# One PSUM tile per accumulator and per h, instead of tiles of two banks, in a fused attention and FFN kernel

## The chip, the cores and the metric

The kernel runs on one core of one Trainium2 chip. The metric is the time of one execution in device microseconds (us). The kernel before takes 1046.71 us in the median of three runs (1044.47 to 1053.35). Its engines are TensorE (PE, with the weight loads shown as PEld), VectorE (DVE), ScalarE (ACT), GpSimd (POOL) and SyncE (SP, which issues the transfers). Matrix products are written by PE into PSUM, eight banks of 512 fp32 per partition; DVE and ACT read them from there.

## The reference

Attention comes first: a pooled form over groups of four positions, repeated to full length, plus a local form with a band of three neighbours on each side. Its result is the input of a feed-forward network.

```python
def _attn_ref(q, k, v):                       # 8 batches x 8 heads x 576 x 64
    q_d, k_d, v_d = (t.reshape(B, H, Sd, 4, D).mean(axis=3) for t in (q, k, v))
    out_up = np.repeat(sm_attn(q_d, k_d, v_d), 4, axis=2)
    scores = np.where(np.abs(pos[:, None] - pos[None, :]) < 4, scale * q @ k.T, -1e9)
    return out_up + softmax(scores) @ v

def _moe_ref(x, w_in, w_out):                 # 4608 tokens, 512 -> 2048 -> 512
    h = x @ w_in
    g = np.where(h >= 1, h, np.where(h <= -1, 0.0, (h + 1) ** 2 / 4))
    return g @ w_out
```

All values are fp32. To keep their precision, each factor of the FFN's two products is held as a high and a low part, so that each product takes three matmuls (high by high, high by low, low by high).

## The kernel before, in words

**Tiling.** The 4608 tokens are cut into chunks: chunk 0 of 512 tokens, chunks 1 to 8 of 384, chunks 9 and 10 of 512. The 2048 inner columns are cut into 16 blocks f of 128. A *step* is one pair (chunk, f). In a step:

- the *first product* (`mm1`, matmuls at line 770) makes h of 128 x 384 or 128 x 512 in one PSUM bank, with 12 matmuls: four blocks of the inner dimension, three each;
- the *gate* (`gates`) makes g from h: ACT copies h from PSUM to m (line 789; in chunk 0 DVE reads h itself), DVE clamps (790), ACT squares (793), DVE combines (796), ACT writes the high part gh (803), POOL the low part gl (806);
- the *second product* (`mm2`, line 824) multiplies g by 128 rows of w_out and adds into the accumulators o0, o1, o2 (and o3 in chunks of 512), one bank each, with three matmuls for each. The accumulators stay in PSUM for the 16 steps of a chunk. After the last (f = 15) ACT copies each to osb (832), and SP sends it out.

**Stages.** Three stages follow one another.

- *First stage*: the attention of the first eight head pairs, the conversion of the weights and chunk 0, in an order written out by hand in the string `ORDER` under `manual_schedule`. A token such as `0.sl@hi1` names an operation and the PSUM tag of its tile; `f3.s2` is a quarter of a first product, `m1.0` the second product of f = 1 into o0.
- *Middle stage*: 128 first products, (1, 1) to (9, 0). The second product follows its first product by two steps: PE does `mm1(k)`, `mm2(k-2)`, `mm1(k+1)`, `mm2(k-1)`, and so on. At 25 places (`JOINS`) the attention of further head pairs is put in: in one step scores and weighted sums on PE (`join`, lines 560 to 615), softmax on DVE, POOL and ACT (631 to 682), and two steps later the transposes on PE (`turn_ps`, 702 and 704) with their copies on ACT (708, 712). These use a tile of four banks.
- *End stage*: the rest of chunks 9 and 10; the second product follows its first by one step. In chunks of 512 its order is o3, o0, o1, o2.

**PSUM before.** The pool `low` is open for the whole kernel, with two tags lo0 and lo1 of two banks each. In the first stage the pool `up` holds hi0 and hi1, in the middle stage `ps_g` takes those four banks, in the end stage `end` holds a new hi0. The function `bank` gives halves of them: h of even f is the first half of lo0, o0 the second half of lo0, o1 and o2 are the halves of lo1, o3 and the h of odd f are the halves of hi0. In the middle stage h is always the first half of lo0.

**Order and waits.** The program's framework tracks which instruction reads and writes which tile, and puts semaphore waits where another engine's earlier access has to be over. Each engine runs its instructions in order. In the middle and end stages the first matmul of each product is held in program order, so that PE's order is as the loops write it. The temporaries m, u, gh, gl and osb share ten buffers under one tag.

Of the kernel before, what the change touches and what calls it, by code (L numbers as in the profile page):

```python
# [9 lines left out]
F32 = mybir.dt.float32  # L10
# [7 lines left out]
P = 128  # L18
# [139 lines left out]
def attention_then_ffn(ctx: ExitStack, tc, qT, kT, vw, vp, vq, band, w_in, w_out, out):  # L158
# [25 lines left out]
    def load(n, name):  # L184

        if n == len(pairs):
            return
        b, p = pairs[n]
        if name in "qk" and n < NPAIR:
            t = wpool.tile([P, 1024], F32, name=f"first_{name}{n}", tag=f"w{'i' if name == 'q' else 'o'}{NFC - NPAIR + n}")  # L190
            nc.sync.dma_start(t[:, 0:S], (qT if name == "q" else kT)[b, p])
        elif name in "qk":
            t = apool.tile([P, S], F32, name=f"{name}_sb", tag=name, bufs=1)
            nc.sync.dma_start(t, (qT if name == "q" else kT)[b, p])
        elif name == "vp" and n < SECOND:
            t = scratch(n, "vp", [KB, 1024])
            nc.sync.dma_start(t, vp[b, p])
        elif name == "vp":
            t = apool.tile([P, FACTOR, P + D], F32, name="vq_sb", tag="vp", bufs=1)
            nc.sync.dma_start(t, vq[b - SECOND // NPAIR, p].rearrange("k (f c) -> k f c", f=FACTOR))  # L200
        else:
            t = scratch(n, "v", [P, NB * D]).rearrange("p (n d) -> p n d", n=NB)
            nc.sync.dma_start(t, vw[b, p].rearrange("k (n d) -> k n d", n=NB))
        loaded[name] = loaded[name, n] = t
# [329 lines left out]
    def pooled_sums(n):  # L534

        state["qd"], state["kd"] = first_qd, apool.tile([P, SD], F32, name="kd", tag="kd", bufs=1)
        for t, name in ((first_qd[:, 0:SD], "q"), (state["kd"], "k")):
            nc.vector.tensor_reduce(
                t, loaded[name].rearrange("p (s f) -> p s f", f=FACTOR), axis=AX.X, op=ALU.add
            )  # L540
# [180 lines left out]
    def load_weights(name, f):  # L721
        t = wpool.tile([P, 512, 2], I32, name=f"raw_{name}{f}", tag=f"w{name}{f}")
        nc.sync.dma_start(t, (w_in if name == "i" else w_out)[f].rearrange("p (n t) -> p n t", t=2))
        raw[name, f] = t
# [4 lines left out]
    def convert(name, f, piece):  # L729

        t = raw[name, f]
        if piece == 1:
            high = t.bitcast(F32)[:, :, 1]
            nc.scalar.activation(high, high, AF.Prelu, scale=2.0**-112, alpha=-(2.0**32))
        elif piece == 2:
            nc.scalar.activation(t[:, :, 0], t.bitcast(U32)[:, :, 0], AF.Copy, scale=2.0**-29)
        elif piece == 3:
            raw["m", name, f] = temp("m")
            mi = raw["m", name, f].bitcast(I32)
            nc.vector.tensor_scalar(mi, t[:, :, 1], 3, None, op0=ALU.logical_shift_left)  # L740
        elif piece == 4:
            mi = raw["m", name, f].bitcast(I32)
            nc.vector.tensor_tensor(mi, mi, t[:, :, 0], op=ALU.add)
        elif piece == 5:
            w = wpool.tile([P, 2, 512], F32R, name=f"w_{name}{f}", tag=f"w{name}{f}")
            nc.scalar.copy(w[:, 0], raw["m", name, f])
            weights[name, f] = w
        else:
            w = weights[name, f]
            nc.gpsimd.tensor_tensor(w[:, 1], raw["m", name, f], w[:, 0], op=ALU.subtract)  # L750

    places = {}
# [28 lines left out]
    def gate(c, f, piece):  # L781

        size = CHUNKS[c][1]
        h = htiles[c, f]
        if piece == "u1":
            utiles[c, f] = temp("u")[:, :size]
            if c > 0:
                m = utiles["m"] = temp("m")[:, :size]
                nc.scalar.copy(m, h)  # L789
            nc.vector.tensor_scalar(utiles[c, f], m if c > 0 else h, -1.0, 1.0, op0=ALU.max, op1=ALU.add)  # L790
        elif piece == "sq":
            u = utiles[c, f]
            nc.scalar.activation(u, u, AF.Square, scale=0.5)  # L793
        elif piece == "u2":
            u = utiles[c, f]
            nc.vector.scalar_tensor_tensor(  # L796
                u, utiles["m"] if c > 0 else h, 1.0, u, op0=ALU.max, op1=ALU.min
            )
        elif piece == "gh":
            gh = mpool.tile([P, 512], F32R, name="gh", tag="t512", bufs=10)[:, :size]  # L800
            gl = mpool.tile([P, 512], F32R, name="gl", tag="t512", bufs=10)[:, :size]
            gtiles[c, f] = gh, gl
            nc.scalar.copy(gh, utiles[c, f])  # L803
        else:
            gh, gl = gtiles[c, f]
            nc.gpsimd.tensor_tensor(gl, utiles.pop((c, f)), gh, op=ALU.subtract)  # L806

    def gates(c, f):
        with tc.high_priority(offset=100):
            for piece in ("u1", "sq", "u2", "gh", "gl"):  # L810
                gate(c, f, piece)
# [25 lines left out]
        for t in (3, 0, 1, 2) if CHUNKS[c][1] == 512 else (0, 1, 2):  # L837
            second_product(c, f, t)

    low = ctx.enter_context(tc.tile_pool(name="low", bufs=1, space=bass.MemoryType.PSUM))  # L840
    banks = {}

    def bank(pool, tag, i):
        if tag not in banks:
            banks[tag] = pool.tile([P, 2, 512], F32, name=f"ffn_{tag}", tag=tag)
        return banks[tag][:, i]

    with tc.tile_pool(name="up", bufs=1, space=bass.MemoryType.PSUM) as up, tc.manual_schedule():
        ops = [first_pairs(n) for n in range(SECOND)]
        ops.append({f"l{x}": lambda x=x: load(SECOND, {"p": "vp"}.get(x, x)) for x in "qkpv"})  # L850
        warm = up.tile([P, 2, 512], F32, name="warm", tag="hi1")
        for _ in range(WARM):
            nc.tensor.matmul(warm[:, 0, 0:P], ident, ident, start=True, stop=True)
        places["h"] = lambda f: bank(up, "hi0", 1) if f % 2 else bank(low, "lo0", 0)
        places["o"] = lambda t: (
            bank(low, "lo0", 1), bank(low, "lo1", 0), bank(low, "lo1", 1), bank(up, "hi0", 0)
        )[t]
        for token in ORDER:
            token, _, tag = token.partition("@")
            whose, what = token.split(".")  # L860
            kind, f = whose[0], whose[1:]
            if kind in "io":
                if what == "ld":
                    load_weights(kind, int(f))
                else:
                    convert(kind, int(f), int(what[1]))
            elif kind == "f":
                c, f = divmod(int(f), NFC)
                if what[1:].isdigit() and what[0] == "s":
                    product(c, f, int(what[1]))  # L870
                else:
                    gate(c, f, what)
            elif kind == "m":
                second_product(0, int(f), int(what))
            elif tag:
                ops[int(whose)][what](low if tag[0] == "l" else up, tag)
            else:
                ops[int(whose)][what]()
    steps = [(c, f) for c in range(1, len(CHUNKS)) for f in range(NFC)]
    first, second = iter(steps[1:]), iter(steps)  # L880
    gates(*steps[0])
    with tc.tile_pool(name="ps_g", bufs=1, space=bass.MemoryType.PSUM) as ps_g:
        places["h"] = lambda f: bank(low, "lo0", 0)
        pooled_sums(SECOND)
        joined = None
        for n in range(NFC + 1, (NMID + 1) * NFC + 1):
            mm1(*next(first))
            if n in JOINS:
                joined = join(SECOND + JOINS.index(n), ps_g)
                next(joined)  # L890
                next(joined, None)
            elif n - 1 in JOINS:
                next(joined, None)
            if n > NFC + 1:
                mm2(*next(second))
            if n - 2 in JOINS:
                next(joined, None)
        mm2(*next(second))
    with tc.tile_pool(name="end", bufs=1, space=bass.MemoryType.PSUM) as end:
        del banks["hi0"]  # L900
        places["h"] = lambda f: bank(end, "hi0", 1) if f % 2 else bank(low, "lo0", 0)
        places["o"] = lambda t: (
            bank(low, "lo0", 1), bank(low, "lo1", 0), bank(low, "lo1", 1), bank(end, "hi0", 0)
        )[t]
        for c, f in first:
            mm1(c, f)
            mm2(*next(second))
        for c, f in second:
            mm2(c, f)
# [65 lines left out]
```

## Time and profile before

| | |
|---|---|
| median of three runs | 1046.71 us (1044.47 to 1053.35) |
| profiled execution | 1048.52 us, span of its trace 1046.7 us |
| PE busy / weight loads | 930.7 us (89%) / 791.4 us (76%) |
| DVE / ACT / POOL busy | 476.1 / 466.6 / 379.0 us |
| mean granted clock of PE | 0.991 |
| first products, 128x384 and 128x512 into lo0, high parts | 310.9 us, 1216 matmuls |
| second products, high parts, into lo0 and lo1 | 332.1 us, 1056 matmuls |

A row of the timeline has start and duration in us, engine, line, operation, the tile written and what it reads, the shape, the number of merged instructions, and in brackets how long the engine sat idle before it and what ended that. A row of the waits has who waited for whom, the sum in us, how often and the longest. A row of the chain has start, duration and what the chain was in. Matmuls are pipelined: each lasts longer than the distance to the next one's start, so rates are read from starts.

### The profile page before, as it was taken

How to read it: one execution, taken by the hardware profiler on the slowest of the kernel's cores; microseconds unless marked ns; L12 is line 12 of the kernel's file. 1: busy time of each engine (PE TensorE's matmuls, PEld its weight loads, DVE VectorE, ACT ScalarE, POOL GpSimd, SP SyncE). 2: the span in 40 equal slices, each digit the busy share in tenths (PEclk: the TensorE clock that was granted, in tenths of full speed). 3: DMA queues.
4: the chain of work that ended last, by engine and by line, in shares of the span. 5: the costliest groups of instructions: out<-in, count | busy, mean ns of one | idle time of the engine just before them, and what ended most of it. 6: DMA issues, size and time to landing. Idle time of an engine off the chain costs nothing.

```text
span 1046.7 us, 18187 instructions
## 1 busy us (share of the span) xinstructions
PE 930.7 (89%) x7444; PEld 791.4 (76%) x7444; DVE 476.1 (45%) x866; ACT 466.6 (45%) x987; POOL 379.0 (36%) x356
## 2 busy tenths in 40 slices
PE   8689999998998999899898899799989989998997
PEld 6577777787877877777787778688877877776775
DVE  5877945654533454354354255545555421211121
ACT  5889844444434434444443344444444432323233
POOL 5566654433422443233233233333333322121211
PEclk9899999999999999999999999999999999999999
DMA  9883103212111111211111011121121000001001
GB/s 286 291 296 134 52 17 110 67 56 77 51 38 43 52 51 51 68 51 51 46 51 52 31 51 51 51 82 51 51 81 52 14 31 1 1 0 41 1 1 40
DMA packets 27970, 68.56 MB, mean 66 GB/s; under 512 B 3248, under 2 KB 3248, under 8 KB 27888
## 3 DMA queue, kind: packets, MB, share of 16 engines
q1 hardware_dynamic: 27888, 67.42, 19.4%
q8 instruction: 58, 0.95, 0.4%
q14 instruction: 24, 0.20, 0.1%
HBM read 57.97 MB, written 9.44 MB: 64 GB/s over the span
## 4 chain that ended last, share of the span: by engine, by line
PE 61%; ACT 13%; issue 10%; DVE 10%; POOL 5%; DMA 0%; POOLq 0%; ACTq 0%; SPq 0%; DVEq 0%
PE ffn_lo L824 26%; PE ffn_lo L770 20%; ACT m L789 6%; PE ffn_hi L770 5%; DVE u L796 4%; POOL sl L638 3%; ACT sp L666 2%; PE ffn_hi L824 2%; POOL gl L806 2%; PE turn_ps L702 1%; ACT sl L664 1%; ACT osb L832 1%; PE turn_ps L704 1%; DVE sl L682 1%; ACT gh L803 1%
## 5 line engine op out<-in xcount | busy, mean ns | idle before, releaser
L824 PE MATMUL ffn_lo<-w_o,gh 128*128 128x512 f32 x1056 | 332.1, 396 | 80.3 <-ACT m L789 59.4
L806 POOL TENSOR_TENSOR gl<-u,gh 128x384 fp32r<-128x384 f32 (+1 forms) x176 | 194.1, 1103 | 569.5 <-ACT gh L803 398.9
L770 PE MATMUL ffn_lo<-xh,w_i 128*128 128x384 f32 (+1 forms) x1216 | 310.9, 338 | 0.8 <-ACT m L789 0.6
L824 PEld LDWEIGHTS ffn_lo<-w_o,gh 128*128 128x128 f32 x1056 | 187.3, 189 | 146.4 <-ACT m L789 97.1
L790 DVE TENSOR_SCALAR u<-m 128x384 f32<-128x384 f32 (+1 forms) x160 | 60.4, 378 | 419.3 <-ACT m L789 419.2
L770 PEld LDWEIGHTS ffn_lo<-xh,w_i 128*128 128x128 f32 x1216 | 217.8, 190 | 12.7 <-ACT m L789 0.9
L770 PE MATMUL ffn_lo<-xl,w_i 128*128 128x384 f32 (+1 forms) x608 | 203.7, 335 | 0.0
L824 PE MATMUL ffn_lo<-w_o,gl 128*128 128x512 f32 x528 | 200.8, 380 | 0.0
L803 ACT CAST gh<-u 128x384 fp32r<-128x384 f32 (+1 forms) x176 | 95.1, 541 | 135.2 <-DVE u L796 133.4
L796 DVE SCALAR_TENSOR_TENSOR u<-m,u 128x384 f32<-128x384 f32 (+1 forms) x160 | 116.0, 725 | 83.8 <-ACT u L793 83.8
L789 ACT COPY m<-ffn_lo 128x384 f32<-128x384 f32 (+1 forms) x144 | 70.4, 489 | 179.9 <-PE ffn_lo L770 179.9
L793 ACT ACTIVATE u<-u 128x384 f32<-128x384 f32 (+1 forms) x176 | 97.5, 554 | 99.7 <-DVE u L790 99.6
L770 PEld LDWEIGHTS ffn_lo<-xl,w_i 128*128 128x128 f32 x608 | 115.2, 190 | 2.5
L824 PEld LDWEIGHTS ffn_lo<-w_o,gl 128*128 128x128 f32 x528 | 100.3, 190 | 14.2
L770 PE MATMUL ffn_hi<-xh,w_i 128*128 128x512 f32 x192 | 59.1, 391 | 0.6 <-DVE u L796 0.6
L529 POOL TENSOR_TENSOR xl<-x,xh 128x576 fp32r<-128x576 f32 (+4 forms) x32 | 44.1, 1386 | 36.2 <-ACT xh L528 36.1
L664 ACT ACTIVATE sl<-sl 128x640 f32<-128x640 f32 x24 | 17.7, 737 | 63.0 <-POOL sl L638 63.0
L770 PEld LDWEIGHTS ffn_hi<-xh,w_i 128*128 128x128 f32 x192 | 37.1, 195 | 6.8 <-DVE u L796 1.4
L824 PE MATMUL ffn_hi<-w_o,gh 128*128 128x512 f32 x96 | 30.3, 397 | 11.6 <-ACT m L789 11.6
L770 PE MATMUL ffn_hi<-xl,w_i 128*128 128x512 f32 x96 | 37.2, 387 | 0.0
L638 POOL TENSOR_TENSOR sl<-sl,mxl 128x640 f32<-128x640 f32 x24 | 30.3, 1261 | 6.0 <-DVE mxl L637 6.0
L824 PEld LDWEIGHTS ffn_hi<-w_o,gh 128*128 128x128 f32 x96 | 16.7, 189 | 19.7 <-ACT m L789 18.0
(146 smaller groups left out, 1014.5 us busy)
## 6 DMA issues: line engine op xcount, KB each, us to landing
v<-vw SPq DMA_DIRECT2D x29, 320.0 KB, 3.0
vq_sb<-vq SPq DMA_DIRECT2D x24, 384.0 KB, 3.1
out<-osb SPq DMA_DIRECT2D x36, 256.0 KB, 2.4
raw_i<-w_in SPq DMA_DIRECT2D x16, 512.0 KB, 8.6
raw_o<-w_out SPq DMA_DIRECT2D x16, 512.0 KB, 9.4
q_sb<-qT SPq DMA_DIRECT2D x28, 288.0 KB, 4.3
k_sb<-kT SPq DMA_DIRECT2D x28, 288.0 KB, 4.9
vp<-vp SPq DMA_DIRECT2D x5, 288.0 KB
```

What stands on the lines that cost most here:

```text
L529: nc.gpsimd.tensor_tensor(xl[:, p, dst], x[:, part], xh[:, p, dst], op=ALU.subtract)
L638: shifted = nc.gpsimd.tensor_tensor(slf, slf, ml.unsqueeze(2).broadcast_to([P, NB, WIN]), op=ALU.subtract)
L664: nc.scalar.activation(slf, slf, AF.Exp, scale=0.125)
L666: nc.scalar.activation(sp[:, i], sp_v[i], AF.Exp, bias=mx[:, j : j + 1], scale=scale, accum_out=sums[:, NB + i : NB + i + 1],)
L770: ins = nc.tensor.matmul(htiles[c, f], wi[:, wt, cc * P : (cc + 1) * P], turns(xt[:, cc, ts]), start=(cc == 0 and xt is xh and wt == 0), s ...
L789: nc.scalar.copy(m, h)
L790: nc.vector.tensor_scalar(utiles[c, f], m if c > 0 else h, -1.0, 1.0, op0=ALU.max, op1=ALU.add)
L793: nc.scalar.activation(u, u, AF.Square, scale=0.5)
L796: nc.vector.scalar_tensor_tensor(u, utiles["m"] if c > 0 else h, 1.0, u, op0=ALU.max, op1=ALU.min)
L803: nc.scalar.copy(gh, utiles[c, f])
L806: nc.gpsimd.tensor_tensor(gl, utiles.pop((c, f)), gh, op=ALU.subtract)
L824: ins = nc.tensor.matmul(o, gt[:, ts], turns(weights["o", f][:, wt, :]), start=f == 0 and n == 0, stop=f == NFC - 1 and n == 2,)
```

## The change

Each accumulator and each h gets a PSUM tile of its own of one bank, made by the new function `single`; the tiles of two banks remain for the attention of the first stage. The pool `low`, open throughout, goes. In the first stage a pool `three` holds the tags lo0, lo1 and hi0 for the attention, and is closed at the first token of the FFN; a pool `six` with h0, h1, o0 to o3 is opened in the place of its banks. The middle stage opens `ps_g` (four banks) and `ffn` (h0, o0, o1, o2), the end stage `end` with six tiles. The gate of step (1, 0) is issued inside the first stage's block. The string `ORDER`, the loops, the operations and their shapes are the same.

```diff
-    low = ctx.enter_context(tc.tile_pool(name="low", bufs=1, space=bass.MemoryType.PSUM))
     banks = {}
 
-    def bank(pool, tag, i):
-        if tag not in banks:
-            banks[tag] = pool.tile([P, 2, 512], F32, name=f"ffn_{tag}", tag=tag)
-        return banks[tag][:, i]
-
-    with tc.tile_pool(name="up", bufs=1, space=bass.MemoryType.PSUM) as up, tc.manual_schedule():
+    def single(pool, *tags):
+        for tag in tags:
+            banks[tag] = pool.tile([P, 512], F32, name=f"ffn_{tag}", tag=tag)
+        places["h"] = lambda f: banks["h1" if f % 2 and "h1" in banks else "h0"]
+        places["o"] = lambda t: banks[f"o{t}"]
+
+    def psum(name):
+        return tc.tile_pool(name=name, bufs=1, space=bass.MemoryType.PSUM)
+
+    with psum("pair") as two, tc.manual_schedule(), ExitStack() as six:
...
-        places["h"] = lambda f: bank(up, "hi0", 1) if f % 2 else bank(low, "lo0", 0)
-        places["o"] = lambda t: (
-            bank(low, "lo0", 1), bank(low, "lo1", 0), bank(low, "lo1", 1), bank(up, "hi0", 0)
-        )[t]
+        three = six.enter_context(psum("three"))
         for token in ORDER:
...
             elif kind == "f":
                 c, f = divmod(int(f), NFC)
+                if not banks:
+                    six.close()
+                    single(six.enter_context(psum("six")), "h0", "h1", "o0", "o1", "o2", "o3")
...
             elif tag:
-                ops[int(whose)][what](low if tag[0] == "l" else up, tag)
+                ops[int(whose)][what](two if tag == "hi1" else three, tag)
...
+        gates(1, 0)
...
-    gates(*steps[0])
-    with tc.tile_pool(name="ps_g", bufs=1, space=bass.MemoryType.PSUM) as ps_g:
-        places["h"] = lambda f: bank(low, "lo0", 0)
+    banks.clear()
+    with psum("ps_g") as ps_g, psum("ffn") as four:
+        single(four, "h0", "o0", "o1", "o2")
...
-    with tc.tile_pool(name="end", bufs=1, space=bass.MemoryType.PSUM) as end:
-        del banks["hi0"]
-        places["h"] = lambda f: bank(end, "hi0", 1) if f % 2 else bank(low, "lo0", 0)
...
+    with psum("end") as end:
+        single(end, "h0", "h1", "o0", "o1", "o2", "o3")
```

On every engine the instructions stand in the same order as before, but for one place on DVE, where two neighbours at the head of the middle stage change places. What differs is the semaphore waits. Two places on PE show how; PE's rows read line, operation, tile written, what it reads (first and second product by the weights w_i and w_o), shape, count, and the engines waited for.

The first place is the last step of a chunk in the middle stage: the end of a first product, the second product with f = 15 into o0, o1, o2, and the start of the next first product. Before (ffn_lo_605 is lo0 with h and o0, ffn_lo_731 is lo1 with o1 and o2):

```order
L770 MATMUL ffn_lo_605<-xl,w_i_601 128x384
L824 MATMUL ffn_lo_605<-w_o_1608,gh 128x512 [waits Activation_49]
L824 MATMUL ffn_lo_605<-w_o_1608,gh 128x512
L824 MATMUL ffn_lo_605<-w_o_1608,gl 128x512 [waits Pool_49]
L824 MATMUL ffn_lo_731<-w_o_1608,gh 128x512 x2
L824 MATMUL ffn_lo_731<-w_o_1608,gl 128x512
L824 MATMUL ffn_lo_731<-w_o_1608,gh 128x512 [waits Activation_49]
L824 MATMUL ffn_lo_731<-w_o_1608,gh 128x512
L824 MATMUL ffn_lo_731<-w_o_1608,gl 128x512
L770 MATMUL ffn_lo_605<-xh,w_i_824 128x384 x2
```

The same place now (ffn_h_1871 is h0; ffn_o_1872, 1873 and 1874 are o0, o1 and o2):

```order
L770 MATMUL ffn_h_1871<-xl,w_i_601 128x384
L824 MATMUL ffn_o_1872<-w_o_1615,gh 128x512 x2
L824 MATMUL ffn_o_1872<-w_o_1615,gl 128x512 [waits Pool_49]
L824 MATMUL ffn_o_1873<-w_o_1615,gh 128x512 x2
L824 MATMUL ffn_o_1873<-w_o_1615,gl 128x512
L824 MATMUL ffn_o_1874<-w_o_1615,gh 128x512 x2
L824 MATMUL ffn_o_1874<-w_o_1615,gl 128x512
L770 MATMUL ffn_h_1871<-xh,w_i_831 128x384 [waits Activation_49]
```

Two waits for ACT are gone: the one at the head of the second product (for the copy of h to m) and the one ahead of o2 (for the copy of o1 to osb). A wait for ACT stands now at the head of the next first product (for the copy of h to m). In steps with other f only the first of the two was there, and has moved in the same way.

The second place is a step of the end stage with even f: before (ffn_hi_8529 is hi0 with o3 and the h of odd f):

```order
L770 MATMUL ffn_lo_605<-xl,w_i_1597 128x512
L824 MATMUL ffn_hi_8529<-w_o_1614,gh 128x512 [waits Activation_49]
L824 MATMUL ffn_hi_8529<-w_o_1614,gh 128x512
L824 MATMUL ffn_hi_8529<-w_o_1614,gl 128x512 [waits Pool_49]
L824 MATMUL ffn_lo_605<-w_o_1614,gh 128x512 [waits Activation_49]
L824 MATMUL ffn_lo_605<-w_o_1614,gh 128x512
L824 MATMUL ffn_lo_605<-w_o_1614,gl 128x512
```

And now (ffn_o_8550 is o3, ffn_o_8547 is o0):

```order
L770 MATMUL ffn_h_8545<-xl,w_i_1604 128x512
L824 MATMUL ffn_o_8550<-w_o_1621,gh 128x512 [waits Activation_49]
L824 MATMUL ffn_o_8550<-w_o_1621,gh 128x512
L824 MATMUL ffn_o_8550<-w_o_1621,gl 128x512 [waits Pool_49]
L824 MATMUL ffn_o_8547<-w_o_1621,gh 128x512 x2
L824 MATMUL ffn_o_8547<-w_o_1621,gl 128x512
```

The waits ahead of o3 for gh and gl remain. The wait ahead of o0, for the copy of this step's h to m, is gone. In steps with odd f it stood ahead of o3 instead (there h lay in hi0), and is gone too.

More of the change, by code (lines that the diff above doesn't have):

```diff
@@ L838, in mm2 @@
             second_product(c, f, t)
-    low = ctx.enter_context(tc.tile_pool(name="low", bufs=1, space=bass.MemoryType.PSUM))
     banks = {}
-    def bank(pool, tag, i):
-        if tag not in banks:
-            banks[tag] = pool.tile([P, 2, 512], F32, name=f"ffn_{tag}", tag=tag)
-        return banks[tag][:, i]
-    with tc.tile_pool(name="up", bufs=1, space=bass.MemoryType.PSUM) as up, tc.manual_schedule():
+    def single(pool, *tags):
[6 more added lines that the diff above has]
+    with psum("pair") as two, tc.manual_schedule(), ExitStack() as six:
         ops = [first_pairs(n) for n in range(SECOND)]
         ops.append({f"l{x}": lambda x=x: load(SECOND, {"p": "vp"}.get(x, x)) for x in "qkpv"})
-        warm = up.tile([P, 2, 512], F32, name="warm", tag="hi1")
+        warm = two.tile([P, 2, 512], F32, name="warm", tag="hi1")
         for _ in range(WARM):
             nc.tensor.matmul(warm[:, 0, 0:P], ident, ident, start=True, stop=True)
-        places["h"] = lambda f: bank(up, "hi0", 1) if f % 2 else bank(low, "lo0", 0)
-        places["o"] = lambda t: (
-            bank(low, "lo0", 1), bank(low, "lo1", 0), bank(low, "lo1", 1), bank(up, "hi0", 0)
-        )[t]
+        three = six.enter_context(psum("three"))
         for token in ORDER:
@@ L898, in attention_then_ffn @@
         mm2(*next(second))
-    with tc.tile_pool(name="end", bufs=1, space=bass.MemoryType.PSUM) as end:
-        del banks["hi0"]
-        places["h"] = lambda f: bank(end, "hi0", 1) if f % 2 else bank(low, "lo0", 0)
-        places["o"] = lambda t: (
-            bank(low, "lo0", 1), bank(low, "lo1", 0), bank(low, "lo1", 1), bank(end, "hi0", 0)
-        )[t]
+    with psum("end") as end:
+        single(end, "h0", "h1", "o0", "o1", "o2", "o3")
         for c, f in first:
```

## The prediction

> **What bounds the kernel now.** I read the page first, for the busiest engine, then the waits of PE over the run, then the chain and the timeline of single steps.
>
> ```profile
> PE 930.7 (89%) x7444; PEld 791.4 (76%) x7444; DVE 476.1 (45%) x866; ACT 466.6 (45%) x987; POOL 379.0 (36%) x356
> ```
>
> PE is busy for 89% of the span and no engine beside it for half of it (PEld is its own weight loads), so the question is what keeps PE idle. The waits of its second products, and one row of its weight loads:
>
> ```profile
> PE ffn_lo L824 <- ACT m L789: 59.4, 103, 0.7
> PE ffn_lo L824 <- ACT osb L832: 17.5, 11, 3.2
> PE ffn_hi L824 <- ACT m L789: 11.6, 16, 0.7
> PEld ffn_lo L824 <- ACT m L789: 97.1, 118, 1.1
> ```
>
> 103 times a second product waits for the copy of h out of the other half of lo0: in the middle stage, in all steps but those where the attention's matmuls stand between. None of these waits is for data: the copy to m belongs to the step whose first product has just ended, and the second product behind it works on g of two steps ago. The chain of waits over one such step, in order of time:
>
> ```profile
> 623.86 2.21 PE ffn_lo L824 x9
> 626.07 1.96 PE ffn_lo L770 x12
> 628.04 0.02 issue
> 628.06 0.49 ACT m L789
> ...
> 628.59 2.21 PE ffn_lo L824 x9
> ```
>
> A step takes 628.59 - 623.86 = 4.73 us, and for half a microsecond of it PE stands still for ACT. How fast PE goes without a wait is read from starts in the timeline, from a second product into a first one:
>
> ```profile
> 604.50 0.59 PE L824 MATMUL ffn_lo<-w_o,gh 128*128 128x512 f32 x2
> 605.15 0.60 PE L824 MATMUL ffn_lo<-w_o,gh 128*128 128x512 f32 x2
> 605.79 0.49 PE L770 MATMUL ffn_lo<-xh,w_i 128*128 128x384 f32 x2
> 606.28 0.49 PE L770 MATMUL ffn_lo<-xh,w_i 128*128 128x384 f32 x2
> ```
>
> Three matmuls of 512 columns take 0.65 us, three of 384 take 0.49 us, and the passage from one product to the other costs nothing extra.
>
> **The change part by part.** The instructions keep their order, so only waits are counted.
>
> *Copy of h, middle stage.* Without the wait a step is 4 x 0.49 + 3 x 0.65 = 3.91 us, 0.82 us less than 4.73. The idle time is 59.4 / 103 = 0.58 us of that; the other 0.25 us is what a restart costs (the last matmul's own length, and the first weight load). 103 x 0.82 = **84.5 us**.
>
> What is late next? The wait that is new stands at the head of the next first product, for the same copy. PE gets there a whole second product (1.95 us) later, and the copy is over 0.55 us after its product. Behind it on PE stands everything, but it has 1.4 us of room. Then gh and gl: a second product needs those of two steps ago, two steps being 7.8 us. Steps with the softmax are the tight ones. Of one, whose first product ends at 601.6, the timeline and the chain show:
>
> ```profile
> 604.38 1.00 POOL L806 TENSOR_TENSOR gl<-u,gh 128x384 fp32r<-128x384 f32 x1 [3.83 <-issue]
> 607.96 0.47 ACT L789 COPY m<-ffn_lo 128x384 f32<-128x384 f32 x1
> 608.48 0.70 PE L824 MATMUL ffn_lo<-w_o,gh 128*128 128x512 f32 x2 [0.57 <-ACT m L789]
> 612.30 0.55 DVE L241 TENSOR_TENSOR sp<-sp,sums 128x384 f32<-128x384 f32 x1
> 612.67 0.48 ACT L789 COPY m<-ffn_lo 128x384 f32<-128x384 f32 x1
> 612.83 1.00 POOL L806 TENSOR_TENSOR gl<-u,gh 128x384 fp32r<-128x384 f32 x1 [1.04 <-ACT gh L803]
> 615.41 0.66 PE turn_ps L702 x6
> ```
>
> gl is ready at 605.38, 3.8 us after its product, and in the next step, with DVE and ACT in the softmax, at 613.83, 5.9 us after the product that the copy at 607.96 follows; both inside 7.8. Two waits go ahead of the transposes (those behind the copies at 607.96 and 612.67), so the transposes would start 1.64 us earlier, at about 613.7. They need sp, last written at 612.85: 0.8 us of room. The first product behind them needs the copy that ends at 613.15, and would start near 614.9: 1.7 us of room. In the sum new stalls count 0; up to 0.3 us for each of 24 attention blocks (7 us) goes into the range.
>
> *Copy of an accumulator.* At the end of a chunk o2 waits until o1 is copied, behind gh on ACT. The real need comes a first product later (1.96 us), when the next chunk writes o0, whose copy ends earlier still. Of 17.5 us in 11 waits the last, of 0.68, is in the tail below: 16.8 + 10 restarts x 0.25 = **19.3 us**.
>
> *Copy of h, end stage.* With even f the accumulator o3 goes first and hides most of the copy; with odd f nothing does:
>
> ```profile
> 872.66 0.38 PE L824 MATMUL ffn_hi<-w_o,gl 128*128 128x512 f32 x1
> 873.12 0.70 PE L824 MATMUL ffn_lo<-w_o,gh 128*128 128x512 f32 x2
> 877.54 0.38 PE L770 MATMUL ffn_hi<-xl,w_i 128*128 128x512 f32 x1
> 878.65 0.70 PE L824 MATMUL ffn_hi<-w_o,gh 128*128 128x512 f32 x2 [0.73 <-ACT m L789]
> ```
>
> From start to start stand 0.46 and 1.11 us where 0.215 would; with 0.11 us for the first pair (0.70 against 0.59) the loss is 0.35 and 1.00. Odd: 16 waits, the last not counted (tail): **15.0 us**. Even: the weight loads wait 118 times, 103 of them above, so 15 x 0.35 = **5.3 us**.
>
> *The tail*, the last second product (o3, o0, o1, wait, o2) and its copies:
>
> ```profile
> 1034.61 0.58 ACT L789 COPY m<-ffn_hi 128x512 f32<-128x512 f32 x1 [2.37 <-PE ffn_hi L770]
> 1039.21 0.48 PE L824 MATMUL ffn_hi<-w_o,gl 128*128 128x512 f32 x1 [0.68 <-POOL gl L806]
> 1040.44 1.18 ACT L832 COPY osb<-ffn_lo 128x512 f32<-128x512 f32 x2
> 1041.67 0.70 PE L824 MATMUL ffn_lo<-w_o,gh 128*128 128x512 f32 x2 [0.68 <-ACT osb L832]
> 1042.68 0.58 ACT L832 COPY osb<-ffn_lo 128x512 f32<-128x512 f32 x1 [1.06 <-PE ffn_lo L824]
> ```
>
> The last gl follows its product by about 4.6 us, whatever PE does between: so the last odd wait brings nothing. (In the steps before, PE needs gl 5.17 + 0.43 = 5.6 us after the product: 1 us of room.) Without the wait for osb the last copy starts at 1041.62, behind the other two: **1.1 us**.
>
> *The clock.* After two long waits PE ran slowly for a while. One, in the chain and in stretches of 5 us (the numbers at the end: granted clock, transfers' share, GB/s):
>
> ```profile
> 947.39 0.70 PE L824 MATMUL ffn_lo<-w_o,gh 128*128 128x512 f32 x2 [2.47 <-ACT osb L832]
> 948.31 4.29 PE ffn_hi L770 x12
> 961.69 2.60 PE ffn_hi L770 x12
> 425.00:430.00 5.00, 4.38 (x22) 3.90 (x21) 0.92 (x2) 2.33 (x5) 0.00 (x0) 0.87 0.11 41
> 950.00:955.00 5.00, 4.27 (x16) 3.29 (x15) 0.94 (x2) 1.21 (x2) 0.00 (x0) 0.81 0.16 57
> ```
>
> 4.29 - 2.60 = 1.7 us, and the same for the stretch at 425: **3.4 us**, if it is the wait that slows PE. [...]
>
> *First stage.* One wait is longer, one goes:
>
> ```profile
> 36.83 0.70 PE L770 MATMUL ffn_lo<-xh,w_i 128*128 128x512 f32 x2
> 37.05 0.74 DVE L490 TENSOR_TENSOR own<-pl_ps,own 128x576 f32<-128x576 f32 x1
> 68.24 0.70 PE L824 MATMUL ffn_lo<-w_o,gh 128*128 128x512 f32 x2 [2.24 <-DVE u L796]
> ```
>
> h0 lies where hi0 was, whose last reader is the DVE row, so PE's first FFN matmul starts at 37.8: 1 us lost. At 68.24 two accumulations (1.3 us) now go ahead of the wait, and the next product into h0 waits. Net 0, between -2 and +2.
>
> Sum: 84.5 + 19.3 + 15.0 + 5.3 + 1.1 + 3.4 + 0 = 128.6 us. The profiled execution took 1048.5 us (span 1046.7), so it becomes 919.9; the median of the runs lies 1.8 us lower: **918 us**.
>
> **The rivals.**
>
> *Softmax sets the pace of the attention blocks.* If sp comes over 0.8 us later than traced (the copies on ACT and the matmuls now collide with it), the excess is lost at each of 24 blocks, up to both waits gained there, 24 x 1.64 = 39 us: 957 us; with half of it, 938. For it: the chain at these places runs through DVE, ACT and POOL already. Against: that chain hangs on the block's own matmuls, which start it no sooner relative to it, and the row at 601 to 613 has its room. 0.08 for about half, 0.05 for all.
>
> *Slower: the clock.* PE would run 747 us (918 less the first 160 and 11 of the tail) with almost no pause. If the granted clock there fell below 747 / (747 + 128.6) = 0.853, the kernel would be slower than before; at the 0.81 of the row above it would take 918 + 747 x 0.23 = 1090 us. Against it: within a step PE runs 4 us without a pause already, and the clock over the 100 us from 600 is full:
>
> ```profile
> 600.00:700.00 100.00, 88.75 (x821) 77.24 (x820) 49.88 (x94) 41.35 (x97) 37.03 (x37) 1.00 0.20 62
> ```
>
> 0.03. [...]
>
> *The waits are not what PE stands on.* If PE, let through, waited at the same places for gh or gl, nothing would change: 1047. The two steps of distance speak against it. 0.02.
>
> **How the numbers follow.** Forecast 0.82 with 918. Its own bounds: new stalls +7, the clock +3.4, the first stage +-2, a step read 0.02 us too short or long (103 times, +-2): 912 to 931. The half case at 938 belongs to the range of 8 in 10: **912 to 938**; outside are the full softmax case, the clock and no change. A run of this kernel tells 1% from no change; faster by more: 0.82 + 0.08 + 0.05 = 0.95; same 0.02; slower 0.03.
>
> **What would show it.** Right: no row of PE's second products waiting for m or osb but for a few; a middle step of 3.9 us in the chain; PE busy near 97% of a shorter span; the end stage's pair of steps 10.3 us instead of 11.7; no drop of the clock after 60 us. Wrong: transposes (702) waiting for DVE's sp, first products (770) waiting for m, join matmuls waiting for the copies at 708 and 712, a granted clock under 0.95, or a step of 3.9 us with matmuls spaced wider than 0.163 and 0.215 us.

## The result and the profile after

The kernel after takes 925.97 us in the median of four runs (922.49 to 927.31), against 1046.43 us before (the three runs above and one more); the ratio is 0.8833, with a 95% interval of 0.8785 to 0.8882. The forecast was 918 us, in a range of 912 to 938. The profiled execution took 924.72 us with a span of 922.9, 123.8 us less than the span before, where the sum of the prediction had 128.6.

The page, and the rows in which PE waits after the change (engine, line and tile, who was waited for, the sum in us, how often, the longest):

```profile
PE 891.7 (97%) x7444; PEld 792.2 (86%) x7444; DVE 477.3 (52%) x866; ACT 460.9 (50%) x987; POOL 380.5 (41%) x356
...
PE tp_ps L438 <- DVE sl L395: 8.4, 2, 6.6
...
PE turn_ps L702 <- DVE sp L241: 1.2, 1, 1.2
PE ffn_h L770 <- ACT m L789: 1.2, 3, 0.6
PE join_ps L560 <- POOL gl L806: 1.1, 2, 0.5
...
PE ffn_h L770 <- ACT osb L832: 0.7, 1, 0.7
...
PE ffn_o L824 <- ACT osb L832: 0.3, 1, 0.3
```

The same instructions, 7444 matmuls, fill 97% of a shorter span. Of the second products' waits for m, 71 us in 119 places before, none is left; for the copies to osb 0.3 us is left of 17.5; the wait for m that is new at the head of the next first product shows three times. A wait of the first product for osb is new as well (0.7 us, at the head of the end stage). The largest row that remains (8.4 us) lies in the first stage and was there before, with 8.1. The chain, first over two steps of the middle stage, then over an even and an odd step of the end stage:

```profile
555.74 1.94 PE ffn_o L824 x9
557.68 1.95 PE ffn_h L770 x12
559.63 1.94 PE ffn_o L824 x9
561.57 1.95 PE ffn_h L770 x12
```

```profile
771.77 2.59 PE ffn_o L824 x12
774.36 2.59 PE ffn_h L770 x12
776.95 2.59 PE ffn_o L824 x12
779.54 2.59 PE ffn_h L770 x12
```

Neither ACT nor "issue" stands between the products any more. A step takes 3.89 us in place of 4.73, a pair of steps at the end 10.36 in place of 11.71. The stretches in which the two places fall now where the clock had dropped, and the whole middle stage (PE busy, PEld, DVE, ACT, POOL, granted clock, transfers' share, GB/s):

```profile
150.00:750.00 600.00, 595.00 (x5383) 543.23 (x5382) 326.20 (x616) 283.93 (x661) 243.71 (x233) 1.00 0.19 63
385.00:390.00 5.00, 5.00 (x33) 4.62 (x32) 2.02 (x4) 3.04 (x7) 1.86 (x2) 1.00 0.04 12
836.00:841.00 5.00, 5.00 (x25) 4.38 (x24) 0.96 (x2) 3.78 (x7) 1.28 (x1) 1.00 0.28 103
```

PE pauses for 5 us of 600, and the clock is full.

Since PE runs the same instructions in the same order in both kernels, the two traces can be laid side by side product by product. The difference by stage, in us (the end stage begins with the first product of step (9, 1), the tail with the last wait of the last second product for gl):

| stage | terms of the prediction | predicted | measured |
|---|---|---|---|
| first stage (to 155.9 us before) | | 0 | -0.3 |
| middle stage | copy of h 84.5, osb 16.6, clock 1.7 | -102.8 | -98.1 |
| end stage | odd 15.0, even 5.3, osb 2.7, clock 1.7 | -24.7 | -24.5 |
| tail | | -1.1 | -0.9 |
| sum | | -128.6 | -123.8 |

### The profile page after: what moved, and what is told of

Same layout as the page of the kernel before. It is cut to its first block, busy times and chain, and to the rows that moved or that the text cites. A ratio compares the mean times of both kernels' runs of the same rounds, so it can differ in the third digit from the quotient of the medians.

```text
span 922.9 us, 18189 instructions
## 1 busy us (share of the span) xinstructions
PE 891.7 (97%) x7444; PEld 792.2 (86%) x7444; DVE 477.3 (52%) x866; ACT 460.9 (50%) x987; POOL 380.5 (41%) x356
## 4 chain that ended last, share of the span: by engine, by line
PE 83%; DVE 6%; ACT 5%; issue 3%; POOL 2%; DMA 1%; POOLq 0%; ACTq 0%; DVEq 0%
PE ffn_h L770 36%; PE ffn_o L824 35%; PE join_ps L572 2%; PE join_ps L587 1%; PE turn_ps L702 1%; PE join_ps L598 1%; PE turn_ps L704 1%; PE join_ps L560 1%; POOL sl L638 1%; DVE u L796 1%; ACT sp L666 1%; PE tp_ps L438 1%; POOL xl L529 1%; ACT osb L832 1%; DMA q_sb<-qT 1%
## 5 line engine op out<-in xcount | busy, mean ns | idle before, releaser
L770 PE MATMUL ffn_h<-xh,w_i 128*128 128x384 f32 (+1 forms) x1408 | 368.3, 343 | 4.0 <-ACT m L789 1.2
L824 PE MATMUL ffn_o<-w_o,gh 128*128 128x512 f32 x1152 | 347.1, 383 | 1.0 <-ACT gh L803 0.7
L770 PEld LDWEIGHTS ffn_h<-xh,w_i 128*128 128x128 f32 x1408 | 252.6, 189 | 23.2 <-ACT m L789 2.3
L770 PE MATMUL ffn_h<-xl,w_i 128*128 128x384 f32 (+1 forms) x704 | 239.9, 341 | 0.5 <-POOL xl L529 0.5
L824 PEld LDWEIGHTS ffn_o<-w_o,gh 128*128 128x128 f32 x1152 | 212.5, 189 | 31.1 <-issue 5.4
L824 PE MATMUL ffn_o<-w_o,gl 128*128 128x512 f32 x576 | 218.8, 380 | 0.9 <-POOL gl L806 0.9
L789 ACT COPY m<-ffn_h 128x384 f32<-128x384 f32 (+1 forms) x160 | 80.2, 501 | 118.8 <-PE ffn_h L770 118.3
L770 PEld LDWEIGHTS ffn_h<-xl,w_i 128*128 128x128 f32 x704 | 133.1, 189 | 6.2 <-POOL xl L529 1.1
L824 PEld LDWEIGHTS ffn_o<-w_o,gl 128*128 128x128 f32 x576 | 109.0, 189 | 17.1 <-POOL gl L806 1.7
L666 ACT ACTIVATE sp<-join_ps,mxp 128x144 f32<-128x144 f32 x72 | 26.9, 380 | 0.0
```

What stands on the lines that cost most here:

```text
L666: nc.scalar.activation(sp[:, i], sp_v[i], AF.Exp, bias=mx[:, j : j + 1], scale=scale, accum_out=sums[:, NB + i : NB + i + 1],)
L770: ins = nc.tensor.matmul(htiles[c, f], wi[:, wt, cc * P : (cc + 1) * P], turns(xt[:, cc, ts]), start=(cc == 0 and xt is xh and wt == 0), s ...
L824: ins = nc.tensor.matmul(o, gt[:, ts], turns(weights["o", f][:, wt, :]), start=f == 0 and n == 0, stop=f == NFC - 1 and n == 2,)
```

## Experiments: one part undone at a time

All four use the kernel after with a `single` that takes groups of tags, each group one tile:

```diff
-    def single(pool, *tags):
-        for tag in tags:
-            banks[tag] = pool.tile([P, 512], F32, name=f"ffn_{tag}", tag=tag)
+    def single(pool, *groups):
+        for group in groups:
+            tags = group.split()
+            tile = pool.tile([P, len(tags), 512], F32, name=f"ffn_{tags[0]}", tag=tags[0])
+            for i, tag in enumerate(tags):
+                banks[tag] = tile[:, i]
```

**h with o0, middle stage only.**

```diff
-        single(four, "h0", "o0", "o1", "o2")
+        single(four, "h0 o0", "o1", "o2")
```

> The kernel after, but in the middle stage h and o0 lie in one tile of two banks, so the second product waits again for the copy of h to m. Theory (the term of 0.82 us a step is right: idle 0.58 and 0.25 for the restart): 926 + about 82 = 1008 us, between 1003 and 1012, with the row of L824 waiting for m back at about 100 times and 59 us, no waits for osb, and no drop of the clock. Rival (only the idle time counts, the 0.25 is how the ends are modelled): 926 + 60 = 986 us. Rival (a part of the gain comes from which banks the tiles lie in, not from the waits): under 980 us.

Measured: 1010.26 us (four runs, 1008.42 to 1012.14), 84 us above the kernel after. In the trace the middle stage is 85.4 us longer, the other stages differ by 1.1 at most. The waits of PE in it:

```profile
PE ffn_h L824 <- ACT m L789: 59.1, 103, 0.7
PE ffn_h L770 <- ACT osb L832: 3.8, 7, 0.9
```

Laid beside the kernel after, the 103 places with these waits cost 86.0 us, 0.84 in most of them, for 59.1 us of idle time. So the price of one such wait is its idle time of 0.57 us and a quarter of a microsecond of restart, as the first term had it; the rival that counted the idle time alone (986) falls, and so does the one that gave a part to the banks (under 980). The waits for osb in the second row cost 4.6 us beside that, and about as much is saved because small waits of the kernel after, described below, don't occur here. No clock drop followed these 0.6 us waits (mean granted clock 0.992 to 0.995 in the four runs, 0.991 to 0.994 in those of the kernel after).

**o1 with o2, middle stage only.**

```diff
-        single(four, "h0", "o0", "o1", "o2")
+        single(four, "h0", "o0", "o1 o2")
```

> The kernel after, but in the middle stage o1 and o2 lie in one tile, so at the end of each chunk o2 waits for the copy of o1 to osb. Theory (these waits cost their idle time and a restart each, as the two traces show: 15.8 us in seven places of the middle stage): 926 + 16 = 942 us, 938 to 944; of it 1.7 us only if the clock drops again after the longest wait. Rival (PE only waits here instead of a little later, so most of it is absorbed): under 932 us.

Measured: 954.56 us (five runs, 948.69 to 957.32), the profiled execution being the shortest. Both theories missed it on the same side. The waits, and two stretches around them:

```profile
PE ffn_o L824 <- ACT osb L832: 22.0, 8, 4.9
```

```profile
243.00:248.00 5.00, 3.67 (x20) 3.48 (x21) 0.20 (x1) 2.35 (x5) 0.99 (x1) 1.00 0.41 157
391.00:396.00 5.00, 3.17 (x13) 2.84 (x14) 0.26 (x1) 2.07 (x4) 0.99 (x1) 0.71 0.29 106
```

Five of these waits were 1.57 us long before and are 2.41 us long here. The copy of o1 stands behind the gate on ACT and ends no earlier, while PE, which no longer stops for h, comes to it 0.84 us earlier. So the two kinds of waits do not add up: what one of them gives depends on whether the other is gone. With both in place the copy to osb cost 15.3 us in seven places; alone it costs 23.0 us in the same seven, and the clock beside it: it dropped behind two of the waits in the profiled execution (mean granted clock 0.993), and the other four have a mean of 0.980 to 0.987.

**The end stage only.**

```diff
-        single(end, "h0", "h1", "o0", "o1", "o2", "o3")
+        single(end, "h0 o0", "o1 o2", "o3 h1")
```

> The kernel after, but the end stage has the tiles of two banks (h0 with o0, o1 with o2, o3 with h1). Theory (in steps of odd f 1.00 us for the copy of h, of even f 0.35, and at the end of chunk 9 the wait for osb; the two traces differ by 25.4 us there, 1.7 of it the drop of the clock): 926 + 24 = 950 us, 947 to 953, the tail 1 us longer. Rival (the o3 that goes first in even steps hides the copy whole, and odd steps lose only the idle 0.73): 926 + 14 = 940 us.

Measured: 946.98 us (four runs, 946.15 to 948.26). In the trace the middle stage is the kernel after's to 0.03 us and the end stage is 22.9 us longer, the tail 0.9: 15.0 us in the odd steps, 5.2 in the even ones, 2.7 for the wait for osb. No clock drop followed that wait (2.47 us idle, as long as the one before that had a drop behind it; mean granted clock 0.995). The theory of 24 us without the drop holds (the time lies at the lower edge of its range, 947 to 953), the rival's 14 doesn't.

```profile
PE ffn_o L824 <- ACT m L789: 11.7, 16, 0.7
PE ffn_o L824 <- ACT osb L832: 3.5, 3, 2.5
```

**Tiles of two banks everywhere, in the new pools.**

```diff
-                    single(six.enter_context(psum("six")), "h0", "h1", "o0", "o1", "o2", "o3")
+                    single(six.enter_context(psum("six")), "h0 o0", "o1 o2", "o3 h1")
...
-        single(four, "h0", "o0", "o1", "o2")
+        single(four, "h0 o0", "o1 o2")
...
-        single(end, "h0", "h1", "o0", "o1", "o2", "o3")
+        single(end, "h0 o0", "o1 o2", "o3 h1")
```

> The kernel after with its new pools in their new places, but tiles of two banks as before in all three stages: every wait of the kernel before is back, only the pools differ. Theory (it is the waits alone): 1046 us, 1042 to 1052, ratio to the kernel before 0.995 to 1.005, the clock dropping again after the longest waits. Rival (the places of the pools matter by themselves): off by more than 1%.

Measured: 1051.42 us (ten runs, 1048.97 to 1053.73) against 1046.0 for the kernel before on the same chip, ratio 1.0033 (1.0005 to 1.0061). The waits of the second products are back with the same sums to 0.1 us. In the profiled executions the first stage was 1.5 us shorter and the middle stage 3.9 us longer: 2.9 us are one more drop of the clock, behind the same wait of 3.18 us that had none in the profiled execution before, and 1.0 is the wait of the first product for osb at the head of the end stage, which this kernel shares with the kernel after. First this kernel, then the kernel before, each around that wait:

```profile
677.00:682.00 5.00, 3.23 (x12) 2.85 (x13) 0.20 (x1) 2.07 (x4) 0.99 (x1) 0.56 0.29 106
```

```profile
679.00:684.00 5.00, 3.76 (x26) 3.64 (x26) 0.00 (x0) 3.00 (x6) 0.99 (x1) 1.00 0.42 156
```

The places of the pools, then, gave nothing and cost this one wait; the whole gain is the waits and what the clock does behind them.

## Experiments: how long a pause slows PE

The clock term (3.4 us) was open: is the drop due to the wait, and how long must the wait be? Two kernels with o1 and o2 in one tile in the middle stage lengthen the waits for the copy of o1, with more copies of it (the second has 5 in place of 2):

```diff
-            nc.scalar.copy(osb, o)
+            for _ in range(2 if t == 1 and 0 < c <= NMID else 1): nc.scalar.copy(osb, o)
```

> As the kernel with o1 and o2 in one tile in the middle stage, but ACT copies o1 twice there (the same copy again), so that each wait at the end of a chunk of the middle stage grows by one copy, about 0.6 us, to an idle time of about 2.2 us in most places and about 3.8 at the longest. If the time is lost in full: that kernel + 7 x 0.6 = 4 us, about 946 us. [...]

> The same with five copies of o1: the idle times grow by 2.4 us, to about 4 us in most places. Lost in full without a drop of the clock: 942 + 7 x 2.4 = 959 us. If idle time slows PE: 1.7 us more at each place where it drops, up to 12 us, so 959 to 971, and the first product behind each wait takes 4.3 us in place of 2.0. If the clock hangs on something else: 959 and no drop.

Measured: 960.66 and 984.39 us, one execution each; both above what was expected, for two reasons. The waits began at 2.4 us and not at 1.6 (above). And the clock dropped behind six of the first kernel's seven long waits and behind all eight of the second's: against the profiled execution with one copy, in which it dropped twice, it cost some 8 us more in the first and 17 in the second (an estimate: half the time at half clock in which PE wasn't idle). A stretch behind one wait of 4.88 us with five copies:

```profile
245.00:252.00 7.00, 5.27 (x15) 5.00 (x16) 0.00 (x0) 2.20 (x4) 0.00 (x0) 0.53 0.29 110
```

For every wait of PE of over 1.2 us behind the first 60 us, the table has whether the granted clock fell in the 18 us that follow (stretches of 2 us). It goes over the profiled executions of both kernels and of all twelve of the experiments, those of the next sections included; one wait of 1.24 us, with a longer one and its drop right behind it, is left out:

| idle time of PE | waits | clock fell behind |
|---|---|---|
| 1.2 to 2.31 us | 42 | 0 |
| 2.40 to 2.7 us | 12 | 6 |
| 3.0 to 3.42 us | 29 | 21 |
| 3.47 to 7.4 us | 15 | 15 |

A drop is to 0.50 and lasts 3.41 us or twice that (10.24 us once, behind the longest wait), so it costs 1.7 or 3.4 us, and less where a part of it falls into a wait of PE. So the waits are the cause, and yet the same wait, as long to 0.01 us, is followed by a drop in one execution and not in another.

What decides is where the wait lies in time. In each of the 14 traces all drops begin at whole multiples of 3.4133 us from one another, to 0.003 us: with two copies they begin at 244.51, 319.60, 398.11, 476.61, 630.21 and 712.13 us, 22, 23, 23, 45 and 24 times that apart. If the time of a trace is cut into stretches of 3.413 us at these instants, the clock dropped behind all 41 waits of the table of which at least 2.02 us fell into one stretch, and behind none of the 55 with 1.95 us or less; of the two between, the wait with 1.99 us had a drop and the one with 2.01 had none. The wait of 3.18 us had 2.05 us in one stretch in the kernel with pairs everywhere, and 1.79 in the kernel before. Read this way, a wait under 2.0 us brings no drop (none of the 42 of up to 2.31 us did), one of 4 us always brings one (an estimate from the 2.0 us and the stretches of 3.413 us; all 15 waits of 3.47 us and more did), and between the two the position decides, which differs from one execution to the next. The 3.4 us that the prediction counted for the two drops of the kernel before were rightly counted. The drops also fit the spread of the kernel before, 1044 to 1056 us with mean granted clocks of 0.995 to 0.982. The kernel after spreads over 922 to 927 us only; behind the first stage the longest wait of PE in its trace is 1.22 us.

## Experiments: how much room is left

The prediction gave the copy of h 1.4 us of room before the next first product, and gh and gl more. Here ACT copies h to m three or five times in each step of the middle stage, which ends the copy 1.0 or 2.0 us later and changes nothing else of the computation:

```diff
-                nc.scalar.copy(m, h)
+                for _ in range(3 if c <= NMID else 1): nc.scalar.copy(m, h)
```

> The kernel after, but in the chunks of the middle stage ACT copies h to m three times: the copy is over about 1.0 us later in each of 128 steps. Theory (1.3 us of room between the copy's end and the next first product, 1 us and more for gh and gl): 926 + 0 to 8 us, losses only in the blocks of attention. Rival (the waits were removed into hardly any room; PE already stands on the copy or on gh and gl): up to 1.0 us in each step without attention, about 100 us more.

> The same with five copies: the copy is over about 2.0 us later, beyond the room of 1.3. Theory: the next first product (L770) waits for m in nearly every step, 0.65 us idle and 0.25 for the restart, about 0.9 x 100 = 90 us, 1000 to 1030 us, the waits of L770 for m showing about 65 us. Rival (the true limit is elsewhere, in ACT's work per step or in gl): the waits stand at L824 for gh or gl, and the time is higher, or there is no loss at all and the time stays under 940.

Measured: 970.46 us with three copies, 1110.54 us with five, one execution each. The waits are where the theory had them, at the first product for m, but three copies cost 45 us in place of 0 to 8 (in the trace 44.9 in the middle stage), and five cost 189 there in place of 90. Of the 189, some 39 are the clock, which dropped 19 times (the estimate is made as above); with three copies it didn't drop (mean granted clock 0.995). The waits, first with three copies, then with five:

```profile
PE ffn_h L770 <- ACT m L789: 32.1, 49, 2.0
```

```profile
PE ffn_h L770 <- ACT m L789: 131.7, 86, 4.4
```

Two steps without attention, with three copies (timeline, the rows of the ring alone; in brackets how long the engine was idle before, and what ended that):

```profile
587.35 1.51 ACT L789 COPY m<-ffn_h 128x384 f32<-128x384 f32 x3
588.97 0.36 DVE L790 TENSOR_SCALAR u<-m 128x384 f32<-128x384 f32 x1 [2.31 <-ACT m L789]
589.36 0.52 ACT L793 ACTIVATE u<-u 128x384 f32<-128x384 f32 x1 [0.50 <-DVE u L790]
589.92 0.56 DVE L796 SCALAR_TENSOR_TENSOR u<-m,u 128x384 f32<-128x384 f32 x1 [0.59 <-ACT u L793]
590.51 0.51 ACT L803 CAST gh<-u 128x384 fp32r<-128x384 f32 x1 [0.62 <-DVE u L796]
591.25 1.51 ACT L789 COPY m<-ffn_h 128x384 f32<-128x384 f32 x3 [0.23 <-PE ffn_h L770]
```

The gate of a step is a ring on ACT: copy, square, gh, with DVE between, and only then the next copy. With three copies it takes 3.67 us of a step of 3.90, and ACT still waits 0.23 us for PE: a plain step has just enough room. With one copy it takes 2.65 us; 1.2 us is left. In a block of attention, though, other work stands in that ring (the rows of these three lines of ACT, and the matmul that waits):

```profile
605.11 0.74 ACT L664 ACTIVATE sl<-sl 128x640 f32<-128x640 f32 x1 [2.41 <-POOL sl L638]
605.75 0.38 ACT L666 ACTIVATE sp<-join_ps,mxp 128x144 f32<-128x144 f32 x1
606.12 0.48 ACT L789 COPY m<-ffn_h 128x384 f32<-128x384 f32 x1
606.48 0.40 ACT L666 ACTIVATE sp<-join_ps,mxp 128x144 f32<-128x144 f32 x1
606.85 0.49 ACT L789 COPY m<-ffn_h 128x384 f32<-128x384 f32 x1
607.21 0.41 ACT L666 ACTIVATE sp<-join_ps,mxp 128x144 f32<-128x144 f32 x1
607.58 0.50 ACT L789 COPY m<-ffn_h 128x384 f32<-128x384 f32 x1
608.13 0.59 PE L770 MATMUL ffn_h<-xh,w_i 128*128 128x384 f32 x2 [0.89 <-ACT m L789]
```

The exponentials of the softmax stand between the copies, and PE waits. To tell the plain steps from the blocks, three copies were put once into the 33 steps outside the blocks and once into the 95 steps inside:

```diff
-                nc.scalar.copy(m, h)
+                for _ in range(3 if c <= NMID and min(abs(2 * (16 * c + f - j) - 3) for j in JOINS) > 3 else 1): nc.scalar.copy(m, h)
```

(the second kernel has `<= 3` in place of `> 3`)

> The kernel after, with three copies of h to m only in the 33 steps of the middle stage that are not within a block of attention (the step of the scores and the three behind it). Three copies in all 128 steps cost 45 us. Theory (the ring copy, clamp, square, combine, gh, and then the next copy, which ACT runs in this order, takes 2.7 us of a step of 3.9, 3.7 with three copies, so it fits in a plain step and fails only where the softmax is on DVE and ACT as well): 0 to 3 us more than the kernel after, no rows of waits for m in the plain steps. Rival (the copy alone has too little room before the next first product, anywhere): 33/128 of the 45 us, 12 us more.

> The counterpart: three copies of h to m only in the 95 steps within a block of attention. Theory (the ring on ACT has no room in the blocks): 42 to 47 us more than the kernel after, 1.8 us for each of 25 blocks, waits of the first product for m as with three copies everywhere. Rival: 95/128 of the 45 us, 33 us more.

Measured: 927.06 and 963.02 us, one execution each, with the kernel after at 922.96 on the same chip (six runs, 922.50 to 924.88, ratio 0.882 to the kernel before; this run stands below with the last experiment). In the traces the middle stage is 3.5 and 39.9 us longer. Both are a little outside the theory's ranges (0 to 3, 42 to 47), and the rival's 12 and 33 are further off; together they make 43.4 of the 44.9 us. The 3.5 us fall in four places: the first step of the stage (1.0), the ends of two chunks (1.0 each), where the copies to osb share the ring, and the transposes of one block (0.3). So a plain step has the room that the ring says, and it is short where other work stands in the ring, in the blocks above all.

## Experiment: other places for the attention

What still waits in the middle stage (5.4 us) comes in the main from the first blocks and from transposes that fall together with the copies at the end of a chunk. Another list of places was to take these away:

```diff
-JOINS = [17, 20, 23, 26, 30, 37, 44, 51, 58, 63, 68, 73, 78, 85, 92, 99, 106, 111, 115, 120, 125]
+JOINS = [18, 21, 24, 27, 30, 37, 44, 51, 57, 62, 67, 73, 78, 85, 92, 99, 105, 110, 115, 120, 125]
```

> The kernel after with another list of places for the attention in the middle stage: 17, 20, 23, 26 become 18, 21, 24, 27, and 58, 63, 68, 106, 111 become 57, 62, 67, 105, 110, so that no transposes fall together with the copies at the end of a chunk. Theory (the 5.3 us that PE still waits in the middle stage come from the late start of the first blocks and from two such coincidences): 2 to 4 us less than the kernel after, 922 to 924 us. Rival (other blocks take over, or the first blocks are late by something that moves with them): the same within 1 us.

> The kernel after itself, unchanged, as the base on the same chip: 926 us, 922 to 928.

Measured: 937.91 us (six runs, 935.40 to 944.49) against 922.96 for the kernel after: 15 us slower, which neither had expected.

```profile
PE ffn_h L770 <- ACT xh L528: 7.0, 2, 3.6
PE ffn_h L770 <- POOL xl L529: 2.7, 4, 1.1
```

The coincidences and their waits are gone (three waits for m, 1.6 us, stand at the start of the stage now), but the list also decides when the tokens of a batch are ready: at two places the first product of a chunk now reaches tokens whose high and low parts are not yet made (7.0 us for xh, 2.2 of the 2.7 for xl), and behind both waits of 3.5 us the clock dropped for 6.8 us, which cost 5.1 us in all (half the time in which PE wasn't waiting). 7.0 + 2.2 + 5.1 = 14.3 us, against 13.8 us by which the middle stage is longer in the trace. The kernel after has little in reserve at such places either (PE waits for xl twice, 0.5 us in all); no version of this study beats it.

The unchanged kernel after, laid beside its first profiled execution, differs by 1.6 us in the first stage, by 0.03 in the middle stage and by 0.01 at the end. All that these two executions differ by lies in the first 155 us.

## Why the prediction was right, point by point

- **False waits for the copy of h, 84.5 us.** Shown: undone alone, the 103 waits cost 86.0 us place by place (0.84 each in most), and the middle stage is 85.4 us longer in all. The step of 3.91 us came out at 3.89.
- **False waits for osb, 19.3 us.** As a difference of the two kernels they gave about 18.5 us without the drops: 15.8 in the middle stage (15.3 in the seven places and 0.5 at its head) and 2.7 in the end stage. The 1.0 us of the eighth chunk's end, which the sum also counted, was lost again: the first product of step (9, 1) now waits 0.75 us for a copy to osb, though the prediction saw the next need only at o0. As a price these waits are no constant: with the others gone they cost 23.0 us in the same seven places.
- **End stage, 15.0 and 5.3 us.** Shown by undoing it: 15.0 and 5.2.
- **Tail, 1.1 us.** 0.9. The last odd wait brought nothing, as worked out: PE waits at o3 for gh (0.71 us) in its place, and for gl as before.
- **First stage, 0.** It came out at -0.3 us. The wait for `own` is new (0.9 us) and the one for u (2.2 us) is gone, as worked out; but kernels with the same first stage took 152.5 to 156.7 us for it in their profiled executions, so its sum is not tested.
- **Clock, 3.4 us.** Right in the profiled execution, and the cause is shown. As a size it belongs to an execution, not to the kernel: how many drops an execution of the kernel before has, and how long ones, hangs on where its waits lie.
- **"In the sum new stalls count 0."** This is the step that failed, inside the 7 us that went into the range for it: the middle stage gained 98.1 us and not 102.8. PE waits there 5.4 us in eleven places, two of which (0.9 us) stood there before. Place by place the new waits cost 5.6 us: the transposes for sp 1.4 in the first block and 1.0 in four others, two joins for gl 1.2, the first product for m at the ends of two chunks 1.1, and the first product for osb at the head of the end stage 0.9. Small gains elsewhere make up the rest.
- **The softmax as the pace.** Its room was put at 0.8 us; the distance from the end of sp to the transposes was 2.4 us before in most blocks and is about 0.7 now, and 0.14 in five of the 24, where PE waits for it. So the rival was near: it cost 2.4 us, not 20 to 39. In four of these five blocks DVE's last operation on sp was itself late. When it began with POOL's gl, to 0.02 us (four blocks), DVE took 0.55 us and POOL 1.4 in place of 1.0; when gl was 0.07 us ahead (the other four), POOL took 1.0 and DVE 1.35, as if one of the two waited for the other. One of each kind:

```profile
268.59 1.43 POOL L806 TENSOR_TENSOR gl<-u,gh 128x384 fp32r<-128x384 f32 x1
268.60 0.55 DVE L241 TENSOR_TENSOR sp<-sp,sums 128x384 f32<-128x384 f32 x1
...
601.14 1.01 POOL L806 TENSOR_TENSOR gl<-u,gh 128x384 fp32r<-128x384 f32 x1
601.22 1.36 DVE L241 TENSOR_TENSOR sp<-sp,sums 128x384 f32<-128x384 f32 x1
```

- **The slower rival, a cut of the clock by denser work,** didn't come: 1.00 over 600 us with 5 us of pause.
- **From the profile to the median.** The prediction took 1.8 us off because the profiled execution of before lay that much above its median. That execution had two drops of the clock, which the sum had already taken out, so the correction may have counted part of them twice (this is argued, not shown); the profiled execution after lies 1.3 us below its median. With the 4.8 us by which the sum was too large this makes the 8 us between 918 and 926.

The rows of the ring show what the prediction missed in its reasoning on gh and gl: it looked at when PE needs them, two steps later, and not at ACT, which can't begin the next copy before it has made this gh. That limit did not bind here, with 1.2 us left in plain steps. It would be the next one.

## What to carry to other kernels

A tile that spans two PSUM banks is one object to the framework that sets the waits: an accumulator beside a temporary makes every reader of the one hold up the writer of the other, so give each its own tile, and look for waits whose releaser works on data that the waiting instruction doesn't read. Cost such a wait by the distance of starts with and without it (here 0.84 us for 0.57 us idle), and don't add up prices of waits that stand one behind the other on one engine. Before moving work into room that a faster engine leaves, follow the in-order ring of the engine that feeds it, at the place where other work shares it: the 33 plain steps took three copies for 3.5 us in all, the attention's 25 blocks lost 1.6 us each.

## What had not been expected of the hardware

The granted clock fell to 0.50 behind pauses of PE from 2.40 us on, behind half of them up to 2.7 us and behind all from 3.47 us on, for up to 1.7 or 3.4 us of lost time. Whether it fell went by how much of the pause lay in one stretch of a grid of 3.413 us: about 2.0 us was enough (it fell behind all 41 waits with 2.02 us or more, behind none of the 55 with 1.95 or less). A pause can so cost nearly twice its own length: the wait of 2.40 us that ended at 422 us in the kernel before cost 2.4 us, 0.25 for the restart and 1.7 for the clock, 4.3 us in all. And DVE's operation of 0.55 us took 1.36 us where a POOL operation had begun 0.07 us ahead of it, and 0.55 where the two began together.
